# Output projection by one level of Strassen's scheme over pairs of token tiles, with more dense work left behind the attention

## The chip, the core and the metric

The kernel runs on one core of a Trainium2 chip. The metric is the time of one execution in microseconds on the device, lower is better. Before the change three runs took 998.38, 996.33 and 998.14 us, median 998.14. Engines are called as in the profile: PE (TensorE, matmuls), PEld (its weight loads), DVE (VectorE), ACT (ScalarE), POOL (GpSimd), and SP, whose queue issues nearly all DMAs.

## What is computed

Two independent halves over S = 2048 tokens and D = 576 features, written side by side to one output of 2048 x 1152, all in float32:

```python
# A: infini-attention, 32 heads of 18, four segments of 512 tokens
q, k, v = x @ wq, x @ wk, x @ wv
for s in range(4):                       # per segment and head
    p = softmax(qs @ ks.T * scale + mask)
    o_s = g * (phi(qs) @ M) / (phi(qs) @ z) + (1 - g) * (p @ vs)
    M, z = M + phi(ks).T @ vs, z + sum(phi(ks))
a = concat(o) @ wo                       # the output projection
# B: Fourier mixing by matrices
y = dft_seq_re @ (x @ dft_hid_re.T) - dft_seq_im @ (x @ dft_hid_im.T)
```

The mask lets a query see the keys at and before its own place.

## The kernel before

The order of all instructions on every engine is the order in which the program is written (manual_schedule). Two generators are woven into each other by hand: attention() yields a planned time for each slot of work (SLOTS), dense() yields a planned time for each few matmuls of half B, and the loop at the end of the kernel takes dense steps while the dense share of its total stays below the attention's share. total_a is the attention's planned time divided by 0.995, so that 0.5% of the dense plan is left when the attention has ended. later(n, fn) puts a call n ticks ahead; a tick passes at each attention slot, and "while due: tick()" empties the list.

Float32 products are made of three rounded ones: a value is split into hi (an ACT copy to fp32r) and lo (a subtraction raw - hi, on DVE or POOL), and hi x lo', hi x hi' and lo x hi' are summed in PSUM. Features come as four blocks of 128 and a tail of 64; the tail's hi and lo share one tile of 128 rows.

The stages in order: projections and memory (up to about 215 us), then attention woven with dense (to about 928 us), a rest of dense, then the output projection. For attention, each group of four heads is transposed by turn_out and written to the DRAM tile od, the last features of four groups by turn_tails to odt; both DMAs go through the SP queue. wo_load and wo_split bring in and split the weight wo in five row blocks during the last dense products (tt of 8 and more, ri = 1).

The output projection is a loop over 16 token tiles of 128 rows. o_load(t) brings tile t from od and odt with three DMAs, o_split(t) makes hi, lo and the tail, and for each half of the columns (288) a chain of 14 matmuls (4 blocks x 3, and 2 for the tail) runs into one PSUM bank, which ACT copies to SBUF (L1025); four DMAs store a tile. Tiles 0 and 1 are loaded inside attention(), at p == NP + 1; tile t + 2 is loaded when tile t is split. Its matmuls have line L84 in the profile (the helper chain), those of dense L583 and L628 to L634.

SBUF tiles come from pools with a number of buffers per tag. "wide" has 32 buffers (weights, and part of the dense intermediate), "ab" ten for the rest of it. sb2a holds the attention's tiles; open_output closes it and opens sb3 in its place.

Of the kernel before, what the change touches and what calls it, by code (L numbers as in the profile page):

```python
# [12 lines left out]
F32 = mybir.dt.float32  # L13
F32R = mybir.dt.float32r
# [3 lines left out]
OP = mybir.AluOpType  # L18
# [5 lines left out]
P = 128  # L24
# [16 lines left out]
def infini_attention_and_fnet(ctx: ExitStack, tc: tile.TileContext, xT, wqk, w8, wv, wo, beta, xtT, cT, hT, out):  # L41
# [13 lines left out]
    od = [dram.tile([4, 4 * P, P], F32, name=f"od{s}") for s in range(NSEG)]  # L55
    odt = [dram.tile([2 * P, P], F32, name=f"odt{s}") for s in range(NSEG)]

    def split(hi, lo, raw, lo_engine=None):
        act.activation(hi, raw, AF.Copy)
        (lo_engine or dve).tensor_tensor(lo, raw, hi.bitcast(F32), OP.subtract)  # L60
# [625 lines left out]
    O, O3, OT, WO, WORAW = {}, [], {}, [], []  # L686

    def o_load(t):  # L690
        if t >= NT:
            return
        s, a = divmod(t, 4)
        o = O3[0].tile([P, 5, P], F32, name="o", bufs=3) if O3 else sb.tile([P, 5, P], F32, name="raw", tag="raw", bufs=3)
        dma(o[:, :4], od[s][:, a * P:a * P + P].rearrange("c p x -> p c x"))
        for i in range(2):
            dma(o[64 * i:64 * i + 64, 4], odt[s][64 * a:64 * a + 64])
        O[t] = o

    def o_split(t):  # L700
        if t >= NT:
            return
        o_load(t + 2)
        o = O.pop(t)
        hi = O3[0].tile([P, 4, P], F32R, name="oth", bufs=2)
        lo = O3[0].tile([P, 4, P], F32R, name="otl", bufs=2)
        tl = O3[0].tile([P, P], F32R, name="ott", bufs=2)
        split(hi, lo, o[:, :4])
        act.activation(tl, o[:, 4], AF.Copy)
        dve.tensor_tensor(tl[64:], o[64:, 4], tl[64:].bitcast(F32), OP.subtract)  # L710
        OT[t] = hi, lo, tl

# [4 lines left out]

    def wo_split(k):
        if k == 0:
            WO.extend(weight(wide_tile(D)))  # L720
        split_wk(WO, k, WORAW.pop(0), 2)

    def open_output():
        p2a.close()
        O3.append(ctx.enter_context(tc.tile_pool(name="sb3", bufs=1, reuse_waits="tile")))

    p2a = ExitStack()
# [179 lines left out]
    def turn_tails(s, u):  # L907
        t = sa.tile([P, 4, 32], F32, name="oglt", bufs=1)
        dve.transpose(t, TAILS[-1])
        later(3, dma, odt[s].rearrange("(p u) x -> p u x", u=2)[:, u], t.rearrange("p q j -> p (q j)"))  # L910

# [9 lines left out]
    def attention():  # L921
        for p in range(NP + V_LAG):
# [90 lines left out]
    for t in range(NT):  # L1013
        o_split(t + 1)
        hi, lo, tl = OT.pop(t)
        y = O3[0].tile([P, D], F32, name="y3", bufs=2)
        for h in range(2):
            cs = slice(h * 288, h * 288 + 288)
            o = ps.tile([P, 288], F32, name="d", bufs=3)
            terms = []  # L1020
            wh, wl, wt1, wt2 = WO
            for k in range(4):
                terms += [(hi[:, k], wl[k][:, cs]), (hi[:, k], wh[k][:, cs]), (lo[:, k], wh[k][:, cs])]
            chain(o, terms + [(tl, wt1[:, cs]), (tl, wt2[:, cs])])
            act.activation(y[:, cs], o, AF.Copy)  # L1025
            if h or t == NT - 1:
                cs = cs if t == NT - 1 else slice(0, D)
                for q in range(4):
                    r = 512 * (t // 4) + P * q + 32 * (t % 4)
                    queue = nc.scalar if h and t == NT - 1 and q >= 2 else nc.sync  # L1030
                    queue.dma_start(out[r:r + 32, cs], y[32 * q:32 * q + 32, cs])

# [4 lines left out]
def _out_features():  # L1037


    f = np.arange(D).reshape(8, 72)  # L1040
    main = f[:, :64].reshape(4, 4, 32).transpose(0, 2, 1)
    return np.concatenate([main.ravel(), f[:, 64:].reshape(2, 32).T.ravel()])

# [29 lines left out]
```

## Time and profile before

| what | value |
|---|---|
| runs | 998.38, 996.33, 998.14 us, median 998.14 |
| profiled execution | span 996.2 us from first to last instruction; what lies outside the span isn't recorded |
| mean granted clock of PE | 0.999 |
| instructions | 25590 |
| DMA | 208.92 MB, mean 210 GB/s |

The page lists, for each engine, the time in which it was busy. A group row reads: line, engine, operation, output <- inputs, shapes, count | total busy us, mean ns of one | idle time just before, and what ended it. A window row gives the length of a stretch, then busy us (and instructions) of PE, PEld, DVE, ACT and POOL in it, the granted clock of PE, the share of DMA and GB/s. A timeline row is start, duration, engine, line, operation, output <- input. A matmul row's duration includes the pipeline behind it, so that the spacing of matmuls is read from how many end in a stretch. The "q" in SPq means the engine's queue, that is, issuing.

### The profile page before, as it was taken

The numbers are of one execution on the slowest core, as the hardware profiler recorded it, in microseconds if no ns is written. First come the engines' busy times: TensorE is split into PE (matmuls) and PEld (weight loads), VectorE is DVE, ScalarE is ACT, GpSimd is POOL, SyncE is SP. The second block draws the span as 40 slices with busy tenths as digits, with TensorE's granted clock in tenths as the row PEclk, the third lists the DMA queues.
The fourth block names the chain that finished last, engine by engine and source line by source line (L and its number), as shares of the span: only waits on it lengthen the run. The fifth ranks groups of instructions, "written<-read, shape, count | busy, mean of one in ns | idle before, by whom it ended". The sixth has DMA issues, their size and how long they took to land.

```text
span 996.2 us, 25590 instructions
## 1 busy us (share of the span) xinstructions
PE 986.1 (99%) x9294; PEld 924.1 (93%) x9294; DVE 753.5 (76%) x2052; ACT 712.0 (71%) x1680; POOL 636.3 (64%) x700
## 2 busy tenths in 40 slices
PE   9999999999999999999999999999999999999998
PEld 8989989899999999999999999999999999999998
DVE  6657667594678777888898888888889899998321
ACT  7757575653887877878788888877777787777243
POOL 2657676675767677666766777766766767667000
PEclk9999999999999999999999999999999999999999
DMA  7537456767588898899999988779999999989455
GB/s 252 187 117 257 172 180 242 234 232 228 150 174 217 215 251 222 207 237 215 245 238 238 222 214 199 178 200 226 230 216 229 238 235 242 240 191 200 128 148 142
DMA packets 305615, 208.92 MB, mean 210 GB/s; under 512 B 206289, under 2 KB 260433, under 8 KB 305489
## 3 DMA queue, kind: packets, MB, share of 16 engines
q1 hardware_dynamic: 305248, 207.15, 80.8%
q8 instruction: 73, 1.20, 0.5%
q14 instruction: 54, 0.43, 0.2%
q10 hardware_dynamic: 240, 0.14, 0.0%
HBM read 121.32 MB, written 57.93 MB: 180 GB/s over the span
## 4 chain that ended last, share of the span: by engine, by line
PE 84%; DVE 6%; ACT 5%; issue 2%; DMA 2%; POOL 1%; SPq 0%; POOLq 0%; DVEq 0%; ACTq 0%
PE d L583 38%; PE s L744 7%; PE d L84 6%; PE v L84 4%; PE pv L862 4%; PE qk L250 4%; PE d L628 3%; PE d L629 3%; PE d L630 3%; PE pv L863 2%; PE m L363 1%; PE t L818 1%; PE qk L84 1%; DVE r L276 1%; PE t L821 1%
## 5 line engine op out<-in xcount | busy, mean ns | idle before, releaser
L750 DVE CUSTOM_DVE_ANT_0 s<-s,causal 128x128 f32<-128x128 f32 (+3 forms) x512 | 248.1, 504 | 94.0 <-PE s L744 84.8
L456 POOL TENSOR_TENSOR clo<-craw,chi 128x512 fp32r<-128x512 f32 x158 | 217.1, 1374 | 94.4 <-ACT chi L451 66.4
L583 PE MATMUL d<-wide,chi 128*128 128x288 f32 x1408 | 261.7, 303 | 0.0
L583 PEld LDWEIGHTS d<-wide,chi 128*128 128x128 f32 x1408 | 210.7, 188 | 2.7 <-issue 1.1
L583 PE MATMUL d<-wide,clo 128*128 128x288 f32 x704 | 173.3, 313 | 0.0
L784 POOL TENSOR_TENSOR hl<-pf,hl 128x768 f16<-128x768 f32 x64 | 112.6, 1759 | 69.3 <-ACT hl L780 58.7
L830 ACT ACTIVATE phi<-t 128x384 f16<-128x384 f32 x128 | 61.8, 483 | 103.8 <-PE t L827 103.8
L744 PE MATMUL s<-ks,qs 108*128 108x128 bf16 (+3 forms) x512 | 132.8, 303 | 2.7 <-DVE negm L750 2.1
L773 ACT ACTIVATE pf<-s,nb 128x128 f32<-128x128 f32 (+3 forms) x256 | 128.3, 527 | 6.2
L583 PE MATMUL d<-ab,chi 128*128 128x288 f32 x640 | 123.3, 302 | 0.0
L845 DVE TENSOR_TENSOR plo<-pf,phi 128x384 f16<-128x384 f32 (+1 forms) x128 | 122.9, 960 | 0.0
L583 PEld LDWEIGHTS d<-wide,clo 128*128 128x128 f32 x704 | 117.8, 189 | 1.9 <-issue 0.5
L451 ACT ACTIVATE chi<-craw 128x512 fp32r<-128x512 f32 x160 | 100.2, 627 | 6.1 <-DMA craw<-xtT 3.3
L831 ACT ACTIVATE pf<-t 128x384 f32<-128x384 f32 (+1 forms) x192 | 99.5, 518 | 5.9 <-PE t L818 5.5
L583 PEld LDWEIGHTS d<-ab,chi 128*128 128x128 f32 x640 | 97.8, 189 | 0.5
L780 ACT ACTIVATE hl<-pf 128x768 f16<-128x768 f32 (+1 forms) x128 | 87.4, 729 | 2.0
L583 PE MATMUL d<-ab,clo 128*128 128x288 f32 x320 | 83.0, 308 | 0.0
L628 PE MATMUL d<-wide,chi 128*128 128x288 f32 x256 | 81.3, 318 | 0.0
L629 PE MATMUL d<-wide,chi 128*128 128x288 f32 x256 | 75.7, 296 | 0.0
L630 PE MATMUL d<-wide,clo 128*128 128x288 f32 x256 | 75.6, 295 | 0.0
L845 POOL TENSOR_TENSOR plo<-pf,phi 128x384 f16<-128x384 f32 x64 | 61.4, 959 | 13.8 <-ACT pf L831 13.3
L784 DVE TENSOR_TENSOR hl<-pf,hl 128x512 f16<-128x512 f32 x64 | 69.4, 1084 | 0.1
(214 smaller groups left out, 2500.1 us busy)
## 6 DMA issues: line engine op xcount, KB each, us to landing
craw<-cT SPq DMA_DIRECT2D x128, 256.0 KB
ks<-kd SPq DMA_DIRECT2D x32, 432.0 KB
qs<-qd SPq DMA_DIRECT2D x32, 432.0 KB
craw<-xtT SPq DMA_DIRECT2D x32, 320.0 KB
vd<-vs SPq DMA_DIRECT2D x16, 440.0 KB
vst<-vd SPq DMA_DIRECT2D x32, 220.0 KB
qd<-p SPq DMA_DIRECT2D x16, 384.0 KB
kd<-p SPq DMA_DIRECT2D x16, 384.0 KB
```

Of the source, the lines that this page charges most:

```text
L84: pe.matmul(o, a, b, start=n == 0, stop=n == len(terms) - 1)
L451: act.activation(hi, raw[:, :4], AF.Copy)
L456: engine.tensor_tensor(lo, raw[:, :4], hi.bitcast(F32), OP.subtract)
L583: pe.matmul(o[h], a, b[:, h * 288:h * 288 + 288], start=start, stop=stop)
L628: pe.matmul(o, xh[:, k], wl[k][:, cs], start=k == 0, stop=False)
L629: pe.matmul(o, xh[:, k], wh[k][:, cs], start=False, stop=False)
L630: pe.matmul(o, xl[:, k], wh[k][:, cs], start=False, stop=False)
L744: pe.matmul(o[:, c:c + w], q[:, i * P:w], k[:, :w], start=True, stop=True)
L750: dve.tensor_tensor_reduce(o[:, c:c + w], o[:, c:c + w], CAUSAL[0][:, L - w:], scale=scale, scalar=-LOWEST, op0=OP.add, op1=OP.min, accum_ ...
L773: act.activation(f[:, FIRST_COL[i]:FIRST_COL[i] + w], o[:, c:c + w], AF.Exp, bias=nb[:, i:i + 1], scale=-1.0)
L784: engine.tensor_tensor(hl[:, 1, a:b], f[:, a:b], hl[:, 0, a:b], OP.subtract)
L845: (pool if kind == 2 else dve).tensor_tensor(lo[:, a:b], f[:, a:b], hi[:, a:b], OP.subtract)
```

## The change

The projection takes token tiles n and n + 8 as one pair, and the two halves of the 576 input features (two blocks of 128 and 32 tail features each) and of the 576 output columns as the other two dimensions. It forms seven products (Strassen's scheme in Winograd's form) instead of eight:

P1 = A11 B11, P2 = A12 B21, P3 = S1 T1, P4 = S2 T2, P5 = S3 T3, P6 = S4 B22, P7 = A22 T4,

where S1 to S4 are sums and differences of blocks of the activations (rows n above, rows n + 8 below) and T1 to T4 of blocks of wo. Each product is a chain of seven matmuls of 288 columns: three for each of two feature blocks, and one for the tails, whose 96 rows hold hi, hi and lo against lo', hi' and hi'. Some products are added in PSUM on top of an earlier one after that has been read.

For this
- the host orders wo differently, in six blocks; wo_split makes B11, B21 and B22 from them;
- the tails of o are copied in DRAM from odt into a new tile ods, four times over, by one more DMA after each turn_tails;
- o_load moves from the attention to open_output and the projection, three DMAs a tile;
- late_weights loads wo again and forms T1 to T4 (LATE) in three rounds, and left(0) forms the activations' blocks of the first pair; both are issued between the steps of the dense rest;
- output_stage runs the seven products of pair n between those of its neighbours, and left(n + 1), for the next pair, is issued between them: on POOL three sums of 384 columns and three low parts of 64 rows, on DVE one difference of 384 columns and seven low parts of 256, on ACT seven copies of 256 and three for the tails; evacuations are two on ACT and five on DVE;
- 0.995 in total_a becomes 0.975.

```diff
-                if ri and 0 <= late < 5:
+                if ri and 0 <= late < 6:
                     wo_load(late)
-                if ri and 1 <= late < 6:
+                if ri and 1 <= late < 7:
                     wo_split(late - 1)
...
+    LATE = ["T2", "T1", "T3", "T4"]
...
+    def o_load(t):
+        s, a = divmod(t, 4)
+        o = O3[0].tile([P, 2, 3, P], F32, name="o", tag="o", bufs=5)
+        for k in range(2):
+            dma(o[:, k, :2], od[s][2 * k:2 * k + 2, a * P:a * P + P].rearrange("c p x -> p c x"))
+        dma(o[:, :, 2], ods[s][a].rearrange("u p x -> p u x"))
+        O[t] = o
+
+    def late_weights():
...
+        load(0)
+        yield
+        for c in range(3):
+            (b11, b12), (b21, b22) = ((r[:, :288], r[:, 288:]) for r in raws.pop(c))
+            t = O3[0].tile([P, 4, 288], F32, name="tt", tag="tmp", bufs=2)
+            pool.tensor_tensor(t[:, 1], b12, b11, OP.subtract)
+            dve.tensor_tensor(t[:, 2], b22, b12, OP.subtract)
+            yield
+            dve.tensor_tensor(t[:, 0], b22, t[:, 1], OP.subtract)
+            yield
+            pool.tensor_tensor(t[:, 3], b21, t[:, 0], OP.subtract)
+            if c < 2:
+                load(c + 1)
+            yield
+            hi = th[:, :, c] if c < 2 else ts
+            act.activation(hi, t, AF.Copy)
+            yield
+            if c < 2:
+                for i in (0, 2):
+                    dve.tensor_tensor(tl[:, i:i + 2, c], t[:, i:i + 2], th[:, i:i + 2, c].bitcast(F32), OP.subtract)
+                    yield
+            else:
+                dve.tensor_tensor(ts[:32], t[:32], ts[:32].bitcast(F32), OP.subtract)
+                yield
+
+    def left(n):
...
+        def main(name, raw):
+            m = new()
+            act.activation(m[:, :2], raw[:, :2], AF.Copy)
+            dve.tensor_tensor(m[:, 2:], raw[:, :2], m[:, :2].bitcast(F32), OP.subtract)
+            LEFT[n, name] = m
+
+        def stack(to, raw):
+            act.activation(to, raw, AF.Copy)
+            pool.tensor_tensor(to[64:], raw[64:], to[64:].bitcast(F32), OP.subtract)
...
+        pool.tensor_tensor(t[:, 0], two[:, 0], two[:, 1], OP.add)
+        main("A11", one[:, 0])
+        stack(sa_[:, :2], one[:, :, 2])
+        yield
+        pool.tensor_tensor(t[:, 1], t[:, 0], one[:, 0], OP.subtract)
+        main("S1", t[:, 0])
+        yield
+        dve.tensor_tensor(t[:, 2], one[:, 0], two[:, 0], OP.subtract)
+        main("S2", t[:, 1])
+        yield
+        pool.tensor_tensor(t[:, 3], one[:, 1], t[:, 1], OP.subtract)
+        main("S3", t[:, 2])
+        yield
+        stack(ss, t[:, :, 2])
+        main("A12", one[:, 1])
+        yield
+        main("A22", two[:, 1])
+        stack(sa_[:, 2], two[:, 1, 2])
+        yield
+        main("S4", t[:, 3])
+        yield
 
     def open_output():
         p2a.close()
         O3.append(ctx.enter_context(tc.tile_pool(name="sb3", bufs=1, reuse_waits="tile")))
+        for t in (0, 8):
+            o_load(t)
+
+    def strassen_product(o, n, x, w, first):
+        m, st = LEFT.pop((n, x)), LEFT.pop((n, x, "s"))
+        hi, lo, ws = WO[w]
+        terms = []
+        for c in range(2):
+            terms += [(m[:, c], lo[c]), (m[:, c], hi[c]), (m[:, 2 + c], hi[c])]
+        for i, (a, b) in enumerate(terms + [(st[:96], ws[:96])]):
+            pe.matmul(o, a, b, start=first and i == 0, stop=True, skip_group_check=True)
...
+        for n in range(8):
+            todo = [(first, n), (second, n), (sixth, n - 1), (third, n), (seventh, n - 1), (fourth, n), (fifth, n)]
+            if n == 7:
+                todo += [(sixth, n), (seventh, n)]
+            if n < 6:
+                o_load(n + 2)
+                o_load(n + 10)
+            prepare = left(n + 1) if n < 7 else iter(())
+            for fn, k in todo:
+                if k < 0:
+                    continue
+                piece = fn(k)
+                next(piece)
+                next(prepare, None)
+                next(piece, None)
...
-        later(3, dma, odt[s].rearrange("(p u) x -> p u x", u=2)[:, u], t.rearrange("p q j -> p (q j)"))
+        later(3, dma, odt[s][u], t.rearrange("p q j -> p (q j)"))
+        later(5, dma, ods[s][:, u].rearrange("b (r i) x -> b r (i x)", r=4),
+              odt[s][u].rearrange("(b r i) x -> b r (i x)", b=4, r=1).to_broadcast([4, 4, 32 * P]))
...
-            if p == NP + 1:
-                o_load(0)
-                o_load(1)
...
-    total_a = (NP + V_LAG) * sum(SLOTS) / 0.995
+    total_a = (NP + V_LAG) * sum(SLOTS) / 0.975
...
+    def before_output():
+        yield from left(0)
+        yield from late_weights()
+        o_load(1)
+        o_load(9)
+
+    ready = before_output()
     for t in d:
         tick()
-        td += t or 0.0
-        if 0 in O and td > total_d - 3000.0:
-            o_split(0)
+        next(ready, None)
     while due:
         tick()
...
+    for _ in ready:
+        pass
+    output_stage()
```

In output_stage, first(n) is P1, second is P4 (S2, T2), third P3, fourth P5, fifth P2, sixth P7, seventh P6; first and fifth are copied out by ACT, the others by DVE, and each pair's result goes out in eight DMAs.

More of the change, by code (lines that the diff above doesn't have):

```diff
@@ L55, in infini_attention_and_fnet @@
     od = [dram.tile([4, 4 * P, P], F32, name=f"od{s}") for s in range(NSEG)]
-    odt = [dram.tile([2 * P, P], F32, name=f"odt{s}") for s in range(NSEG)]
+    odt = [dram.tile([2, P, P], F32, name=f"odt{s}") for s in range(NSEG)]
+    ods = [dram.tile([4, 2, P, P], F32, name=f"ods{s}") for s in range(NSEG)]
     def split(hi, lo, raw, lo_engine=None):
@@ L679, in dense @@
                     h_split(1, late - 1)
-                if ri and 0 <= late < 5:
+                if ri and 0 <= late < 6:
                     wo_load(late)
-                if ri and 1 <= late < 6:
+                if ri and 1 <= late < 7:
                     wo_split(late - 1)
                 yield from sequence(ri, tt)
[L686 to L711, printed above, removed]
+    O, O3, LEFT, WORAW, Y3 = {}, [], {}, [], {}
+    WO = {}
+    LATE = ["T2", "T1", "T3", "T4"]
     def wo_load(k):
@@ new lines, in wo_split @@
+        a, b, stacks_ = WO["all"]
+        raw = WORAW.pop(0)
+        if not half:
+            raw = raw[:, :288]
+        if c < 2:
+            hi, lo = (b[0][c], b[1][c]) if half else (a[0][:, c], a[1][:, c])
+            act.activation(hi, raw, AF.Copy)
+            later(2, dve.tensor_tensor, lo, raw, hi.bitcast(F32), OP.subtract)
+        else:
+            st = stacks_[1] if half else stacks_[0][:, :288]
+            act.activation(st, raw, AF.Copy)
+            later(2, dve.tensor_tensor, st[:32], raw[:32], st[:32].bitcast(F32), OP.subtract)
@@ L1004, in infini_attention_and_fnet @@
     open_output()
+    def before_output():
[4 more added lines that the diff above has]
+    ready = before_output()
     for t in d:
         tick()
-        td += t or 0.0
-        if 0 in O and td > total_d - 3000.0:
-            o_split(0)
+        next(ready, None)
     while due:
         tick()
[L1013 to L1031, printed above, removed]
+    for _ in ready:
+        pass
+    output_stage()
 _INS = ("xT", "wqk", "w8", "wv", "wo", "beta", "xtT", "cT", "hT")
```

90 lines of the change are left out of this document (85 added, 5 removed).

## The prediction

> **What bounds the kernel now.** I read the busy times first, then the wait list of PE, then the same busy times by stretches of the span.
>
> ```profile
> PE 986.1 (99%) x9294; PEld 924.1 (93%) x9294; DVE 753.5 (76%) x2052; ACT 712.0 (71%) x1680; POOL 636.3 (64%) x700
> ```
>
> ```profile
> PE s L744 <- DVE negm L750: 2.1, 5, 0.8
> ```
>
> ```profile
> 800.00:900.00 100.00, 98.81 (x1066) 92.42 (x1064) 93.55 (x253) 77.31 (x178) 71.06 (x77) 1.00 0.91 219
> ...
> 920.00:940.00 20.00, 20.00 (x183) 19.86 (x183) 8.04 (x22) 4.34 (x11) 2.95 (x4) 1.00 0.44 119
> ...
> 980.00:990.00 10.00, 10.00 (x78) 10.00 (x77) 1.97 (x4) 3.80 (x10) 0.00 (x0) 1.00 0.59 155
> ```
>
> PE sets the time: its longest listed wait adds up to 2.1 us, so every matmul less is time less, as long as the others keep up. In a window row the columns are length, PE, PEld, DVE, ACT, POOL, clock. Late in the attention DVE is 94% busy; in the output projection DVE and ACT are 20% and 38% busy and POOL does nothing. The chain of waits then gives the two stretches that change:
>
> ```profile
> 928.01 4.33 PE d L583 x32
> 932.34 59.42 PE d L84 x448
> ```
>
> After the attention's last matmul 32 dense matmuls are left (4.33 us); then the projection's 448 take 59.42 us, so 0.1326 us each.
>
> **What it removes.** Eight pairs of tiles, seven products each, seven matmuls per product: 8 x 7 x 7 = 392 instead of 448, all 288 columns wide as before. 56 x 0.1326 = 7.4 us less. The projection's PE floor is 52.0 us, one product 0.93 us, one pair 6.5 us.
>
> **What it moves.** 0.995 becomes 0.975 in total_a, so 2% more of total_d (453.8 us by the code's own 120 ns and 95 ns) stays behind the attention: 9.1 us by that count, 76 matmuls of 120 ns, and 76 x 0.1326 = 10.0 us on the chip. From the attention's last matmul to the end of the dense products it is now 4.3 + 10.0 = 14.3 us. PE's work is only reordered, at no cost, while the attention can run the 10 us denser. DVE at 93.55 of 100 would go to about 95; I take 1 us of new waits (0 to 5, from the 1.2 us PE idles there now). The eight new transfers into ods each make SP wait for odt to land before the transposes and loads behind it can be issued; 8 x 1.8 us of queue. I price it at 0, since SP runs ahead of its consumers there; without that cover it is at most the 14 us. wo comes in six row blocks instead of five, three of them split over half their width: one load more, and no more work on ACT and DVE.
>
> **The first pair: what must happen in those 14.3 us.** Zero is the last attention matmul, at 927.83 here.
>
> ```profile
> 927.83 0.18 PE L863 MATMUL pv<-vst,ptt 128*128 128x37 bf16 x1
> ```
>
> ```profile
> 929.72 0.50 DVE L897 STREAM_TRANSPOSE ogt<-og 128x128 f32<-128x128 f32 x2
> 930.14 0.28 DVE L909 STREAM_TRANSPOSE oglt<-ogl 128x128 f32<-128x128 f32 x1
> ```
>
> ```profile
> 930.65 0.38 SPq L94 DMA_DIRECT2D odt<-oglt  x1
> 931.09 0.44 SPq L695 DMA_DIRECT2D o<-od  x1
> 931.58 1.15 SPq L697 DMA_DIRECT2D o<-odt  x2
> ...
> 971.38 0.38 SPq L695 DMA_DIRECT2D o<-od  x1
> 971.81 1.20 SPq L697 DMA_DIRECT2D o<-odt  x2
> 973.10 1.92 SPq L1031 DMA_DIRECT2D out<-y  x4
> ```
>
> ```profile
> 974.41 0.63 ACT L59 ACTIVATE oth<-o 128x512 fp32r<-128x512 f32 x1 [0.77 <-DMA o<-od]
> ```
>
> Before, tiles 0 and 1 were loaded during the attention. Now the first loads are written behind the attention's last transfers on the same SP queue: od, odt, and the new ods, which has to wait until odt has landed. A load lands 1.4 us after its issue ends (973.01 to 974.41, where ACT waited for it). So: odt issued by +3.2, landed +4.6, ods issued (0.4) +5.0, six issues for tiles 0 and 8 (two of 0.4 and one of 0.55 each, 2.7) +7.7, landed +9.1. Only then can POOL add the first two blocks. The durations:
>
> ```profile
> L653 DVE TENSOR_TENSOR y<-y,d 128x288 f32<-128x288 f32 x32 | 14.1, 445 | 2.2 <-PE d L583 2.2
> ...
> L60 DVE TENSOR_TENSOR otl<-o,oth 128x512 fp32r<-128x512 f32 x14 | 9.7, 692 | 38.6 <-ACT oth L59 38.6
> ...
> L710 DVE TENSOR_TENSOR ott<-o,ott 64x128 fp32r<-64x128 f32 x14 | 4.1, 289 | 1.2 <-ACT ott L709 0.8
> ```
>
> ```profile
> 917.51 1.29 POOL L456 TENSOR_TENSOR clo<-craw,chi 128x512 fp32r<-128x512 f32 x1
> ```
>
> ```profile
> L458 POOL TENSOR_TENSOR xtail<-craw,xtail 64x128 fp32r<-64x128 f32 x30 | 14.8, 492 | 2.4
> ```
>
> ```profile
> L780 ACT ACTIVATE hl<-pf 128x768 f16<-128x768 f32 x64 | 54.0, 844 | 2.0
> ...
> L1025 ACT ACTIVATE y<-d 128x288 f32<-128x288 f32 x32 | 12.8, 411 | 35.3 <-PE d L84 26.9 <-DMA out<-y 5.3 <-ACT ott L709 3.1
> ...
> L59 ACT ACTIVATE oth<-o 128x512 fp32r<-128x512 f32 x14 | 8.8, 628 | 3.2 <-DMA o<-od 3.2
> ```
>
> On straight lines through these, DVE takes 0.42, 0.46, 0.56, 0.76 and 1.36 us for 256, 288, 384, 576 and 1152 columns; POOL 0.49, 0.76, 0.82, 1.03, 1.29 for 128, 256, 288, 384, 512; ACT 0.41 for 256, 1.17 for 1152.
>
> - left(0) on POOL: three sums of 384 columns and stacks of 256, 512 and 128: 3 x 1.03 + 0.76 + 1.29 + 0.49 = 5.6. With 1.3 of waiting behind DVE (next part): +16.0.
> - late_weights, first block of rows: POOL 0.82, DVE 0.46, POOL 0.82: +18.1. The raw blocks are loaded by then.
> - The second block can't run beside the first, since the DVE queue holds its differences behind the first one's low parts: ACT 1.17, DVE 2 x 0.76, DVE 2 x 0.46, POOL 0.82 = 4.4: +22.5. The third likewise: +26.9. Then ACT 1.17 and DVE 1.36: +29.4.
>
> The product with S2 and T2 is second on PE, which reaches it at 14.3 + 0.93 = +15.2. It waits 14.2 us, and everything on PE is queued behind it. From both sides: all three blocks overlapped, POOL alone being the limit, is 9.1 + 5.6 + 6 x 0.82 + 2.5 = +22.1, a wait of 6.9; with no overlap at all of the three engines in left(0) (ACT and DVE add 4 us) about 18. I take 14.2, since each link is an in-order queue.
>
> **The other pairs: DVE and POOL exclude each other.**
>
> ```profile
> 810.79 1.65 POOL L784 TENSOR_TENSOR hl<-pf,hl 128x768 f16<-128x768 f32 x1 [0.19 <-ACT hl L780]
> 812.40 1.09 POOL L835 TENSOR_SCALAR_AFFINE_SELECT pf<-pf 128x512 f32<-128x512 f32 x1
> ```
>
> ```profile
> 811.00 1.99 DVE L845 TENSOR_TENSOR plo<-pf,phi 128x512 f16<-128x512 f32 x1
> ...
> 814.79 0.69 DVE L784 TENSOR_TENSOR hl<-pf,hl 128x512 f16<-128x512 f32 x1
> ```
>
> ```profile
> 907.33 0.63 POOL L835 TENSOR_SCALAR_AFFINE_SELECT pf<-pf 128x512 f32<-128x512 f32 x1
> ```
>
> A DVE difference of two SBUF tiles that takes 0.69 alone took 1.99 when it started under a POOL instruction: it ended 0.55 us after POOL did (812.44 to 812.99). The POOL instruction behind it took 1.09 instead of 0.63. They take turns, so their durations add up and don't overlap.
>
> One left(n) needs, of such work, DVE 7 x 0.42 + 0.56 = 3.5 and POOL 5.6: 9.1 us. Each hand-over gains 0.14 (0.55 against 0.69), at most 13 times, so 7.3 to 9.1; I take 8.4, nearer the upper end, because of the dependencies (sum, difference, copy, low part) between the three. The Trainium skill's page "SBUF — State Buffer", section "Who interferes with whom", speaks against the change more strictly: a VectorE instruction with two SBUF inputs and a GpSimd instruction that reads SBUF exclude each other, and the second is blocked until the first has wholly finished. By that no hand-over gains anything, 9.1 us per pair; the trace agrees on the exclusion and shows the 0.14 besides. PE needs 6.5 per pair. Alone, the engines would fit: POOL 5.6, DVE 3.5 + 5 x 0.45 = 5.75, ACT 5.0 (nine copies of at most 0.63 and two of 0.41). SP fits: six loads 2.7 and eight stores 3.8 make 6.5, all inside 8.4. left(1) starts when POOL has left the weights, at +26.9; left(7) ends at 26.9 + 7 x 8.4 = +85.7; the last pair has nine products, 8.4: +94.1. The stores behind the last product are as before.
>
> **The sum.** On the same zero the old projection would end at 14.3 + 59.4 = +73.7. Difference +20.4, in which the 7.4 us saved are contained. With 1 us for the denser attention and 1 for the clock:
>
> ```profile
> 994.00:995.00 1.00, 0.00 (x0) 0.00 (x0) 0.00 (x0) 0.00 (x0) 0.00 (x0) 0.92 0.19 55
> 995.00:996.20 1.20, 0.00 (x0) 0.00 (x0) 0.00 (x0) 0.00 (x0) 0.00 (x0) 0.50 0.00 0
> ```
>
> the clock falls to half about 3 us after the last matmul, so a 14 us wait loses it; the three products after it take up to 2.8 us longer, but PE is not the bound there; 0 to 2.8. The span would go from 996.2 to 1018.6. The page gives nothing outside the span; the runs lie 0.1 to 2.2 us above it, their median 1.9; 1018.6 + 1.9 = 1020.5, rounded to 1020.
>
> **Rivals.**
> - Preparation hidden (the other side). The loads aren't held behind odt: 2.7 of issue and 1.4 of landing make +4.1 instead of +9.1, and DVE and POOL run side by side, the three weight blocks too. Then T2 comes at 22.1 - 5 = +17.1, a wait of 1.9 against 7.4 saved: 998.1 - 5.5 = 992.6. It decides only if both hold; without the early loads the wait of 6.9 leaves 997.6, no change. For it: each engine alone is under 6.5 us per pair. Against it: the order on SP and the rows at 811.
> - Wait, but no exclusion: the output is bound by PE after +29.4. 998.1 + 14.2 - 7.4, with 1 for the attention: 1006. For it: hand-overs overlap; against it: 7.3 is still over 6.5.
> - Harder on both sides: 9.1 per pair (7 x 0.7 = 4.9 more) and 5 us instead of 1 lost in the denser attention, where DVE has 6% left: 1020 + 8.9 = 1029.
> - The clock doesn't come back. If the gaps of about 2 us in each pair keep it at 0.5, 55 products of 1.86 end at 29.4 + 102 = +132: 1057. Against it: in the rows above it held for 3 us of idleness. "TensorE: Matmul & The Clock Gate" of the Trainium skill, section "A second HAM failure mode: psum-queue depth-cycling", describes a kernel whose frequent short idles did cost it its clock; no run shown here has such gaps.
> - That it does less than it says: the count of 392 is in the loops, so only a wait can undo it.
>
> **How the numbers follow.** Forecast 0.59 (own range 1012, with 7.3 per pair, to 1026); no exclusion 0.16; harder 0.07; hidden 0.15 (0.12 faster, 0.03 no change); clock 0.03. 0.2%, or 2 us, is what these runs can tell from nothing. Faster 0.12, same 0.03, slower 0.85. The range takes in the forecast, the second and the third rival: 1003 to 1031.
>
> **What would show it.** 392 projection matmuls, still 0.13 us each where they are back to back. A PE wait of some 14 us before the second product, ended by DVE (ts), with the clock at 0.5 behind it. The first o load issued after ods. A period of about 8.4 us between first products, DVE differences of 256 columns at 0.42 free and over 0.8 under POOL. A period of 6.5 would prove the exclusion harmless; no long wait before T2 would prove the chain wrong, and both together the forecast.

## The result and the profile after

| | before | after |
|---|---|---|
| median of five runs beside each other | 998.05 us (996.33 to 998.38) | 1031.69 us (1029.87 to 1034.27) |
| ratio, 95% interval | | 1.0346 [1.0332, 1.036] |
| the profiled execution, its span | 996.2 us (span) | 1033.57 us, span 1031.9 |
| last attention matmul starts at | 927.83 us | 923.39 us |

The change makes the kernel 3.5% slower. The forecast was 1020.0, 22 us slower, with a range up to 1031; it came out 34 us slower, 0.7 us above the range. First the busy times of the page, then the list of PE's waits, both of the kernel after:

```profile
PE 990.2 (96%) x9238; PEld 922.6 (89%) x9238; DVE 804.4 (78%) x2135; ACT 721.4 (70%) x1715; POOL 689.1 (67%) x754
```

```profile
PE d L584 <- ACT chi L452: 13.0, 2, 10.6
PE t L824 <- DVE ts L763: 4.2, 1, 4.2
PE t L824 <- DVE u L859: 4.0, 6, 0.9
PE pv L1038 <- DVE plo L1020: 2.1, 1, 2.1
```

PE has 56 matmuls fewer (9294 to 9238) and yet more busy time, in part because some of them ran at half clock. DVE and POOL are 51 and 53 us busier. The list of waits, which had nothing above 2.1 us, now holds 13.0 us in the *dense* products (line 584), 4.2 us before the end of the projection's second product, and 4.0 us spread over the pairs.

The window rows answer to the 920 to 940 and 980 to 990 rows of before (columns: length, PE, PEld, DVE, ACT, POOL, clock):

```profile
930.00:940.00 10.00, 1.63 (x13) 1.40 (x11) 1.10 (x3) 1.25 (x3) 1.99 (x3) 0.78 0.62 193
940.00:950.00 10.00, 5.11 (x24) 4.53 (x24) 7.45 (x9) 4.68 (x10) 7.12 (x7) 0.71 0.35 94
950.00:960.00 10.00, 5.72 (x37) 5.03 (x37) 5.78 (x9) 2.60 (x5) 5.94 (x6) 0.97 0.25 73
960.00:970.00 10.00, 8.54 (x46) 8.19 (x47) 9.01 (x15) 5.04 (x16) 6.77 (x7) 0.69 0.59 174
...
980.00:990.00 10.00, 9.23 (x67) 8.75 (x67) 9.41 (x18) 5.62 (x17) 6.75 (x8) 1.00 0.57 155
```

From 930 to 960 PE executes 74 matmuls, which back to back would take 10 us; DVE and POOL are both near idle for the first 10 us of it and are busy for 5.8 to 7.5 us of each 10 afterwards. Where the pairs run (980 to 990), DVE is busy 9.41 of 10 us, POOL 6.75, and the clock is full.

PE's timeline shows what it waited in. These are the rows of the start-up:

```profile
942.21 1.33 PE L584 MATMUL d<-wide,chi 128*128 128x288 f32 x4 [10.57 <-ACT chi L452]
943.84 0.85 PE L584 MATMUL d<-wide,clo 128*128 128x288 f32 x2 [0.31 <-POOL clo L457]
...
950.07 0.79 PE L584 MATMUL d<-ab,chi 128*128 128x288 f32 x4 [2.45 <-ACT chi L452]
...
961.18 0.61 PE L824 MATMUL t<-ts,x 96*128 96x288 f32 x1 [4.19 <-DVE ts L763]
```

The 14.3 us of dense matmuls that were to cover the preparation stood still themselves. Their last two operands are still to be cut when the attention ends (high part on ACT, line 452, low part on POOL, line 457), and the loop that issues the dense steps advances left(0) and late_weights by one piece per step, so these cuts stand in the ACT and POOL queues *behind* preparation pieces that wait for the o loads. The same on POOL and on ACT:

```profile
937.85 0.99 POOL L789 TENSOR_TENSOR ss<-o 128x384 f32<-128x384 f32 x1 [10.96 <-DMA o<-ods]
...
942.23 1.56 POOL L457 TENSOR_TENSOR clo<-craw,chi 128x512 fp32r<-128x512 f32 x1 [0.20 <-ACT chi L452]
...
950.10 1.33 POOL L457 TENSOR_TENSOR clo<-craw,chi 128x512 fp32r<-128x512 f32 x1 [1.79 <-ACT chi L452]
```

```profile
935.63 0.42 ACT L774 ACTIVATE x<-o 128x256 fp32r<-128x256 f32 x1 [13.73 <-DMA o<-od]
...
941.54 0.61 ACT L452 ACTIVATE chi<-craw 128x512 fp32r<-128x512 f32 x1
...
949.41 0.61 ACT L452 ACTIVATE chi<-craw 128x512 fp32r<-128x512 f32 x1
```

SP's queue shows why the loads were late:

```profile
927.92 0.41 SPq L95 DMA_DIRECT2D odt<-oglt  x1
929.74 0.68 SPq L95 DMA_DIRECT2D ods<-odt  x1
930.47 0.94 SPq L725 DMA_DIRECT2D o<-od  x2
...
933.07 0.47 SPq L726 DMA_DIRECT2D o<-ods  x1
```

SP waited for odt to land, as forecast, issued ods at 929.74 and then the loads of tiles 0 and 8; the last issue ended at 933.54. But POOL began only at 937.85, so this load took 4.3 us to land, not the 1.4 us of the row that the forecast used.

The queue was late before that too. The issue of odt ended 4.9 us after the start of the last attention matmul (928.33 after 923.39), where the forecast had 3.2, as in the kernel before. DVE shows why:

```profile
924.50 0.45 DVE L654 TENSOR_TENSOR y<-y,d 128x288 f32<-128x288 f32 x1 [6.19 <-PE d L584]
924.87 0.21 DVE L1050 RECIPROCAL pv<-pv 128x8 f32<-128x8 f32 x1
```

With the denser weaving a subtraction of the dense product, which waits for PE, stands in DVE's queue ahead of the attention's last normalisation (line 1050). That starts 1.48 us after the last attention matmul; in the kernel before it was 0.22 (928.05 after 927.83). A second such subtraction (line 654, at 926.54) comes ahead of the transposes. Experiment 11, where only the weaving is denser, has the same two; experiment 1, with the old weaving, has odt's issue end at +3.2.

**Where the 35.7 us of span went.** Each line is measured minus forecast, from the rows here and in the prediction:

| stretch | forecast | measured | difference |
|---|---|---|---|
| last attention matmul, due at 927.83 − 10.0 = 917.83 | +1 | 923.39: +5.6 | +4.6 |
| from there to T2 complete (the ts matmul at 961.18) | 29.4 | 37.8 | +8.4 |
| from there to the last matmul's end (1023.25) | 64.7 | 62.1 | −2.6 |
| from there to the end of the span | 4.5, as before | 8.65 | +4.2 |
| clock, counted apart | 1 | within the others | −1 |

The sum is 13.6 us, against 1031.9 − 1018.6 = 13.3. The two rows of the last stretch, the end of PE's work before (991.74 of 996.2) and after:

```profile
991.32 0.42 PE L84 MATMUL d<-wide,ott 128*128 128x288 f32 x2
```

```profile
1022.15 1.10 PE L824 MATMUL d<-wide 128*128 128x288 f32 x7
...
1020.91 8.94 SPq L831 DMA_DIRECT2D out<-yo  x12
```

The SP row merges 12 stores and hides a wait among them. SP's own list of waits (total, times, longest; from 1012 us on) has it, and SP's and ACT's timelines behind it show the stores that were left:

```profile
SPq L831 <- DMA out<-yo: 3.5, 1, 3.5
```

```profile
1025.35 4.51 SPq L831 DMA_DIRECT2D out<-yo  x10
```

```profile
1023.77 0.82 ACTq L831 DMA_DIRECT2D out<-yo  x2
```

SP stood for 3.5 us until another store had landed, and then issued ten stores at 0.45 us each. By the trace's semaphores the store it waited for is one of the last two, which ACT's queue issued at 1023.77. Eight of SP's ten had their data by 1022.81.

### The profile page after: what moved, and what is told of

It reads as the page before. It is cut to its first block, busy times and chain, and to the rows that moved or that the text cites. A ratio compares the mean times of both kernels' runs of the same rounds, so it can differ in the third digit from the quotient of the medians.

```text
span 1031.9 us, 25691 instructions
## 1 busy us (share of the span) xinstructions
PE 990.2 (96%) x9238; PEld 922.6 (89%) x9238; DVE 804.4 (78%) x2135; ACT 721.4 (70%) x1715; POOL 689.1 (67%) x754
## 4 chain that ended last, share of the span: by engine, by line
PE 74%; DVE 8%; ACT 6%; issue 4%; DMA 3%; POOL 3%; SPq 1%; POOLq 0%; DVEq 0%; ACTq 0%
PE d L584 34%; PE s L919 7%; PE v L85 4%; PE pv L1037 4%; PE qk L251 4%; PE d L629 3%; PE d L630 3%; PE d L631 3%; PE pv L1038 2%; PE m L364 1%; PE t L993 1%; PE qk L85 1%; DVE r L277 1%; ACT qe L220 1%; DMA craw<-xtT 1%
## 5 line engine op out<-in xcount | busy, mean ns | idle before, releaser
L584 PEld LDWEIGHTS d<-wide,chi 128*128 128x128 f32 x1408 | 212.6, 190 | 13.6 <-ACT chi L452 10.8
L1020 POOL TENSOR_TENSOR plo<-pf,phi 128x384 f16<-128x384 f32 x64 | 60.9, 951 | 16.4 <-ACT pf L1006 13.6
L959 DVE TENSOR_TENSOR hl<-pf,hl 128x512 f16<-128x512 f32 x64 | 64.3, 1005 | 0.0
```

Of the source, the lines that this page charges most:

```text
L584: pe.matmul(o[h], a, b[:, h * 288:h * 288 + 288], start=start, stop=stop)
L959: engine.tensor_tensor(hl[:, 1, a:b], f[:, a:b], hl[:, 0, a:b], OP.subtract)
L1020: (pool if kind == 2 else dve).tensor_tensor(lo[:, a:b], f[:, a:b], hi[:, a:b], OP.subtract)
```

## The experiments

Theory: the excess over the old time is four things. A: the attention loses about 5 us by being denser. B: a chain of preparation holds up PE at the start, about 38 us from the last attention matmul to T2. C: DVE and POOL exclude each other, which makes a pair 7.8 us instead of 6.5. D: the store queue adds 4 us at the end, in which that wait of SP is 3.5. The main rival to B: the rest of dense work held back in front of the chain is what costs, and clear issue order would hide the preparation. "T2 complete" below is the start of the matmul that reads ts, counted from the last attention matmul of the same profile, unless it says otherwise. The kernel before ran beside each, at medians between 997.5 and 998.4. In the profiles of kernels with the same denser attention its last matmul fell anywhere from 919.96 to 926.87 us, so a difference of 2 us between two of these kernels says nothing unless the trace has its place.

**1. No denser attention** (after, with the old factor):

```diff
-    total_a = (NP + V_LAG) * sum(SLOTS) / 0.975
+    total_a = (NP + V_LAG) * sum(SLOTS) / 0.995
```

> Only total_a goes back from 0.975 to 0.995. Chain theory (everything behind the attention's last matmul hangs on one chain of loads, left(0) and late_weights that starts there, so that the last attention matmul sets the end and not the amount of dense rest): the last attention matmul comes near 927.5 instead of 923.4, 4 us later; the two cuts of craw for the dense rest, which stood in the middle of the chain, fall away and give 3 to 4 back; 1031 to 1035 us. Density theory (the denser attention itself loses the time): 5 to 6 us less, 1026. Cover theory (the rest hides the preparation): 10 us more, 1042.

1035.36 us, ratio 1.0367 [1.0352, 1.0383], 0.4 us above what the chain theory expected. The attention ends at 928.15, as before within 0.3 us, and T2 comes at 963.43 (+35.3). PE's waits in this kernel:

```profile
PE t L824 <- DVE tl L760: 14.7, 2, 11.5
PE s L824 <- ACT x L774: 6.1, 1, 6.1
```

The wait is longer and lies in the projection itself. So the 10 us of dense work moved behind the attention are worth 3.7 us by the medians, 2.1 by the ratios, whose intervals just overlap: the chain B is there with or without it.

**2. The dense rest first** (no piece of the preparation until all dense steps are issued):

```diff
     for t in d:
         tick()
-        next(ready, None)
```

> The whole dense rest is issued ahead of left(0) and late_weights, nothing else is changed. Chain theory: PE no longer waits for the craw copies (13 us in the profile), the rest ends near 938, but the product with T2 still waits for the chain, which gets shorter by the two POOL subtractions of craw and the wait for their ACT copies only: 3 to 5 us less, 1027 to 1029. Rival (the 13 us in which PE stood in the dense rest are themselves the loss): 1018 to 1020.

1028.14 us, 1.029 [1.0273, 1.0307], as expected. The rest runs without a gap and its last matmul starts 14.3 us after the last attention matmul (935.83 after 921.53), but PE then stands in the second product:

```profile
947.41 0.61 PE L824 MATMUL t<-tl,x 128*128 128x288 f32 x1 [9.41 <-DVE tl L760]
...
951.67 0.61 PE L824 MATMUL t<-tl,x 128*128 128x288 f32 x1 [3.18 <-DVE tl L760]
...
956.52 0.61 PE L824 MATMUL t<-ts,x 96*128 96x288 f32 x1 [3.76 <-DVE ts L763]
```

T2 complete at +35.0 instead of +37.8. The rest standing still was a symptom: with the rest ahead, the same wait stands behind it, one for each row block of T2. It is this picture that the prediction had drawn, with 16.4 us of waits in place of 14.2.

**3. No late weights** (the four T's replaced by blocks of wo that exist, so the sums of weights aren't made):

```diff
-        yield from late_weights()
+        for n, b in zip(LATE, ("B11", "B21", "B22", "B11")):
+            WO[n] = WO[b]
+        yield
```

> late_weights is left out; T1 to T4 are taken to be blocks of wo that are there already, so the products are those of other matrices. Chain theory: no wait for T; the pairs start when the dense rest and left(0) are done, near 949 to 951 instead of 961, and take their 62 us as before: 1020 to 1022. If the exclusion of DVE and POOL alone set the time, so that left(1) to left(7) would be late anyway: over 1028.

1022.55 us, 1.0237 [1.0222, 1.0252]: 9 us off the kernel after, just over what was expected. PE still stands 10.3 us in the dense rest (`ACT chi`), which is the loads' part of B; the weights' part is the 9 us.

**4. POOL without reads** (in left(1) to left(7) each POOL sum and low part is replaced by two memsets of the same output, so these operands are constants):

```diff
+        def sums(to, a, b, op):
+            if n == 0:
+                pool.tensor_tensor(to, a, b, op)
+            else:
+                for _ in range(2):
+                    pool.memset(to.bitcast(F32), 0.25)
...
-        pool.tensor_tensor(t[:, 0], two[:, 0], two[:, 1], OP.add)
+        sums(t[:, 0], two[:, 0], two[:, 1], OP.add)
```

> In left(1) to left(7) every POOL sum and low part is replaced by two memsets of the same tile, which write and don't read, and keep POOL about as busy; the values are then constants. Exclusion theory: DVE's 256-column subtractions take 0.42 throughout instead of up to 1.4, a pair takes 6.5 to 6.8 us instead of 7.8, the whole 7 to 9 us less: 1023 to 1025. Rival (the pace comes from the dependencies among the three engines, or from SP): a pair stays over 7.5 us and the time within 2 us of 1031.7.

1026.4 us, 1.0274 [1.0255, 1.0292]. The DVE groups by line from the first pair on, first of the kernel after, then of this one (count, busy time, mean ns):

```profile
L775 DVE TENSOR_TENSOR wide<-ss,wide 128x256 fp32r<-128x256 f32 x28 | 18.2, 651 | 0.6 <-ACT wide L774 0.2
L775 DVE TENSOR_TENSOR wide<-o,wide 128x256 fp32r<-128x256 f32 x21 | 17.9, 853 | 1.8 <-ACT wide L774 1.8
L796 DVE TENSOR_TENSOR ss<-o 128x384 f32<-128x384 f32 x7 | 7.0, 1005 | 0.0
```

```profile
L782 DVE TENSOR_TENSOR wide<-ss,wide 128x256 fp32r<-128x256 f32 x28 | 11.8, 420 | 8.0 <-ACT wide L781 7.7
L782 DVE TENSOR_TENSOR wide<-o,wide 128x256 fp32r<-128x256 f32 x21 | 8.8, 420 | 3.4 <-ACT wide L781 3.4
L803 DVE TENSOR_TENSOR ss<-o 128x384 f32<-128x384 f32 x7 | 3.9, 550 | 0.3 <-issue 0.3
```

With POOL no longer reading, every one of the 49 differences takes 0.42 us; beside a reading POOL they took 0.65 and 0.85 on average. The period between pairs (from one third product, P3, to the next) fell from 7.8 to between 6.5 and 6.6 for five intervals, PE's own 6.5, and was 7.8 again in the last. The memsets also wait for no input, so part of the shorter period can come from a shorter chain of dependencies; the shorter DVE durations can't. So DVE is slowed by the exclusion, and the engines have time enough.

What then set the last interval is SP's queue. It issued each pair's six loads and eight stores without a pause, and took 6.9 to 7.0 us for them (loads begin at 984.07, 991.11 and 997.97), more than PE's 6.5, until a load came late and held up ACT. By these rows a pair without the exclusion would settle near 7 us, an estimate:

```profile
1002.49 0.42 ACT L786 ACTIVATE wide<-o 128x256 fp32r<-128x256 f32 x1 [1.75 <-DMA o<-ods]
```

From T2 to the last matmul's end it is 54.1 us instead of 62.1, but SP's wait among the last stores grew from 3.5 to 4.9 us, about as much as the 1.4 us above the upper expectation.

**5. Loads ahead of ods** (experiment 2, and the last ods transfer held back until the preparation is issued):

```diff
-        later(5, dma, ods[s][:, u].rearrange("b (r i) x -> b r (i x)", r=4),
-              odt[s][u].rearrange("(b r i) x -> b r (i x)", b=4, r=1).to_broadcast([4, 4, 32 * P]))
+        copy = (dma, ods[s][:, u].rearrange("b (r i) x -> b r (i x)", r=4),
+                odt[s][u].rearrange("(b r i) x -> b r (i x)", b=4, r=1).to_broadcast([4, 4, 32 * P]))
+        if s == 3 and u == 1:
+            HELD.append(copy)
+        else:
+            later(5, *copy)
...
+        for fn, *a in HELD:
+            fn(*a)
```

> On top of e2 (dense rest first, 1028.1): the last transfer into ods is held back until left(0) and late_weights have been issued, so that the first o loads no longer stand behind it. Chain theory: 1.4 us of waiting for odt, 0.7 of issue and up to 3 of slow landing beside its 16 KB packets fall away, POOL's first sum starts about 9 us after the last attention matmul instead of 14.5, and all that hangs on it comes 4 to 5 us sooner: 1023 to 1024.5. If the loads land late whatever stands ahead of them: within 1.5 us of 1028.

1029.21 us, 1.0312 [1.0281, 1.0343]: no gain, where 4 us or more were expected. One half held: POOL's first sum began 10.3 us after the last attention matmul (926.87) instead of 14.1 in experiment 2. The other half is in DVE's timeline:

```profile
940.70 0.45 DVE L654 TENSOR_TENSOR y<-y,d 128x288 f32<-128x288 f32 x1 [9.64 <-PE d L584]
...
941.88 0.42 DVE L775 TENSOR_TENSOR x<-o,x 128x256 fp32r<-128x256 f32 x1
```

With the whole rest issued first, its subtraction from PSUM (line 654) stands in DVE's queue ahead of left(0), and it waits for PE to finish the rest. DVE idled 9.64 us, for the last 3.5 of them with all blocks landed. The attention also ended late in this profile, 5 us after that of experiment 2.

**6. Four last stores on ACT's queue** (experiment 2, first half of the last tile):

```diff
-            queue = nc.scalar if last and q >= 2 else nc.sync
+            queue = nc.scalar if first or last and q >= 2 else nc.sync
...
-                store(n, Y3[n][0], C)
+                store(n, Y3[n][0], C, first=True)
```

> On top of e2: four of the last pair's twelve stores (those of the fifth product) are issued by ACT's queue instead of SP's. Theory of the tail (between the last matmul and the end lie 8.6 us instead of 4.4, because SP issues one store in about half a microsecond and has some ten of them behind the last products): 2 us less, 1026. Rival (the stores are late by their data): no change.

1026.0 us, 1.0279 [1.0258, 1.0301], 2.1 us under experiment 2, as expected, though the two intervals overlap. From the end of PE's work to the end of the span it is 7.3 us instead of 8.6 (1023.2 − 1015.9 against 1026.4 − 1017.8), so 1.3 us of D were SP's queue of these four stores; its wait stays, at 3.7 us. In this profile the attention ended 1.6 us earlier besides.

**7. Two more POOL operations on DVE** (experiment 2; in left(n), n ≥ 1, the first sum and the low part of the stacked S tails):

```diff
-        pool.tensor_tensor(t[:, 0], two[:, 0], two[:, 1], OP.add)
+        (dve if n else pool).tensor_tensor(t[:, 0], two[:, 0], two[:, 1], OP.add)
...
-        stack(ss, t[:, :, 2])
+        stack(ss, t[:, :, 2], dve if n else pool)
```

> On top of e2: in left(1) to left(7) one of POOL's three sums and its 512-column low part go to DVE, which does both in less time (0.56 + 0.69 against 1.03 + 1.29). Exclusion theory: the time in which the two need the shared path falls from 9.1 to 8.0 us per pair, DVE's own work rises from 5.75 to 7.0; a pair takes about 7.2 instead of 7.83, 3 to 5 us less: 1023 to 1025. Rival (DVE is simply the busier engine and sets the pace): more work on DVE makes a pair longer, over 8.5, 1033 or more.

1027.78 us, 1.0287 [1.0257, 1.0318]. The period is 7.35 instead of 7.82, close to the 7.2 expected: work is shorter on DVE, and a POOL operation that is gone excludes nothing. The time as a whole missed: in the profile the attention ended at 923.89, 2.4 us after that of experiment 2, and hid most of the gain, which was 2.2 us from T2 to the last matmul's end (59.1 instead of 61.3).

**8. Weights ahead of left(0)** (experiment 5; half of the reload of wo goes out during the last dense product but one, late_weights runs first):

```diff
+                if ri and late == 6:
+                    for i in range(3):
+                        later(4 + i, early_load, i)
...
-        yield from left(0)
-        yield from late_weights()
+        yield from late_weights()
+        yield from left(0)
```

> On top of e5: half of the second load of wo goes out some 10 us sooner, during the last dense product but one, and late_weights is issued ahead of left(0), into the time in which the engines waited for the o loads. Chain theory: late_weights starts about 3 us after the last attention matmul and is done 13 to 14 us later, left(0) overlaps its end; the second product comes near 942 instead of 956.5, and the whole takes 1013 to 1017. If the preparation weren't one serial chain from the loads on: no less than e5, 1023.

1029.66 us, 1.0313 [1.0289, 1.0337]: no gain, where 1013 to 1017 was expected. It is experiment 5's fault again, and now it holds up the weights: DVE waited 9.64 us for the same subtraction, and PE waited 12.2 us for left(0) (`ACT x L772`).

**9. The cuts first, then the preparation** (experiment 5, with the preparation issued right behind the rest's last cut, so ahead of its subtractions):

```diff
-    for t in d:
+    for i, t in enumerate(d):
         tick()
+        if i == 17:
+            for _ in ready:
+                pass
```

> As e5, but the preparation isn't behind the whole dense rest: it is issued once the rest's last cut of craw has been issued, so that DVE's preparation stands ahead of the two last subtractions of the dense product, which wait for PE. In e5 DVE stood 9.6 us in front of those. Chain theory: POOL's first sum about 10 us after the last attention matmul, T2 ready 20 to 21 us later, at +31 instead of +35 in e2: 4 us less than e2, 1023 to 1025. If the first loads don't carry the chain: 1027 or more.

1024.79 us, 1.0275 [1.0261, 1.0289], as expected. T2 complete at +31.0 (953.09 after 922.14), the expected place:

```profile
943.98 0.61 PE L824 MATMUL t<-tl,x 128*128 128x288 f32 x1 [6.32 <-DVE tl L760]
...
948.24 0.61 PE L824 MATMUL t<-tl,x 128*128 128x288 f32 x1 [3.17 <-DVE tl L760]
...
953.09 0.61 PE L824 MATMUL t<-ts,x 96*128 96x288 f32 x1 [3.76 <-DVE ts L763]
```

So both parts of experiment 5's reading hold: the loads' 4 us are there once no queue has something late in front of the chain. The prediction had +29.4, but with 1.8 us for ods in front of the loads, which this kernel doesn't have there: like for like it is +31.0 against +27.6. Of these 3.4 us, 2.8 lie ahead of POOL's first sum (+10.1 against +7.3) and 0.6 in the preparation itself (20.9 against 20.3).

**10. Cuts first, weights ahead of left(0)** (experiments 8 and 9 together):

> As e8 (late_weights ahead of left(0), its first loads sooner), with the order of e9, so that DVE is free for it. Chain theory: the weights start on POOL about 7 us after the last attention matmul, behind the last cuts, are done near +20, and left(0) makes S2 and its tail by +24 to +26; the second product ends near 947 instead of 956.9 in e2: 1017 to 1020. If it stays over 1025, the start isn't one chain that can be begun sooner.

1022.57 us, 1.0256 [1.0242, 1.027], 2.6 us above what was expected. The weights start at +6.8 and are ready about 20 us after the last attention matmul; left(0) is now last, and PE waits for it:

```profile
943.46 0.85 PE L828 MATMUL s<-wide,x 128*128 128x288 f32 x2 [4.54 <-ACT x L772]
```

Its 14th product matmul is at +25.6 (949.89 after 924.33), where +24 to +26 was expected; what was missed is that the attention ended 2.2 us later in this profile than in experiment 9's, and that the second product's evacuation then waits longer (`DVE u L853`, 3.0 us).

**11. The kernel before, denser attention alone**:

```diff
-    total_a = (NP + V_LAG) * sum(SLOTS) / 0.995
+    total_a = (NP + V_LAG) * sum(SLOTS) / 0.975
```

> The kernel before with 0.975 in total_a and nothing else of the change: the attention woven denser, 10 us more of dense work behind it, projection as it was. Density theory (the attention, run denser, meets waits of DVE and POOL on each other and loses 3 to 5 us of PE's time and clock): 1000 to 1003. Rival (order costs nothing, what was lost there in the changed kernel comes from the new transfers): 997.5 to 999.

1002.76 us, 1.0055 [1.0042, 1.0067], as expected: denser weaving costs about 5.5 us by itself (0.0055 of 997.5), with nothing of Strassen in it. Its chain of waits shows the dense rest, 108 matmuls instead of 32, run through without a gap, so that nothing is lost behind the attention:

```profile
922.77 14.42 PE d L583 x108
937.19 59.43 PE d L84 x448
```

The loss lies in the attention. One piece of it has a place, the same in the kernel after, whose DVE and POOL rows near 532 us are:

```profile
530.32 1.86 DVE L127 TENSOR_TENSOR wide<-raw,wide 64x576 fp32r<-64x576 f32 x1
532.21 2.11 DVE L128 TENSOR_TENSOR wide<-raw,wide 64x576 fp32r<-64x576 f32 x1
...
534.35 1.01 DVE L1020 TENSOR_TENSOR plo<-pf,phi 128x512 f16<-128x512 f32 x1
```

```profile
530.30 1.27 POOL L457 TENSOR_TENSOR clo<-craw,chi 128x512 fp32r<-128x512 f32 x1 [2.38 <-ACT nb L945]
531.77 1.93 POOL L959 TENSOR_TENSOR hl<-pf,hl 128x768 f16<-128x768 f32 x1 [0.20 <-ACT hl L955]
533.66 1.16 POOL L1010 TENSOR_SCALAR_AFFINE_SELECT pf<-pf 128x512 f32<-128x512 f32 x1
```

Two low parts of a weight load, 576 columns each (0.76 us by the prediction's line), took 1.86 and 2.11 us between POOL's reads; the low part of the attention behind them came late, and PE idled 2.1 us at 533.3, the `plo` wait of the list. In the kernel after and in this one the clock was at 0.5 for 3.4 us afterwards. That is up to 2.1 + 1.7 = 3.8 us of the 5; the rest has no single place.

**12. All that helped** (experiments 10, 7 and 6 together):

> All parts together: e10, with one sum and one low part moved to DVE (e7) and the last pair's first stores on ACT's queue (e6). If the parts add: 1018.5 less 3.3 (seven periods of 7.35 instead of 7.83) less 2: 1011 to 1015, still over the 998 of before, since a pair takes 7.35 us here against 7.43 by the plain scheme and the start-up wait is not gone.

1017.55 us, 1.0204 [1.0189, 1.022], 2.5 us above what was expected, but 5.0 us under experiment 10 (5.3 expected), so the miss is experiment 10's. It is 14 us better than the change as made, and 20 us slower than the kernel before. None of the kernels tried beats the kernel before. Of experiment 12's 19.7 us of span (1015.9 against 996.2), the dense products end 4.4 us later than before (936.7 against 932.3) and the stretch behind them is 15.3 us longer (79.2 against 63.9), though its eight pairs at 7.35 us take no longer (58.8) than the 448 plain matmuls (59.4). What remains is the start-up and the stores.

## Why the prediction came out as it did

*The direction held, and the mechanism in its outline.* 392 projection matmuls at 0.13 us back to back; a first pair that waits for T2, though 13.0 us of PE's wait lay in the dense rest and only 4.8 before the second product; pairs set by DVE and POOL; a clock that falls to 0.5 and comes back. The rivals "preparation hidden" and "no exclusion" are out: experiments 2 and 9 have the wait, experiment 4 the exclusion. "The clock doesn't come back" is out: it was at 0.5 from 935.5 to 945.7 and from 959.4 to 966.2, and full from there to the end of PE's work.

*"Harder on both sides" came nearest in time (1029), but half by the wrong price.* Its 5 us for the denser attention were right; its 9.1 us per pair weren't.

1. **The denser attention, forecast 1 us: about 5.** The term failed in size. It was read from DVE's mean share (93.55 of 100, to 95 at most), and a mean says nothing of a place where two DVE operations and POOL's reads meet. Experiment 11 measures it alone. The transfers into ods, priced at nothing within the attention, cost nothing there that shows (experiment 1 has them and ends the attention as before).
2. **The first pair's chain, forecast +29.4: +37.8.** 5.4 of the 8.4 us lie ahead of POOL's first sum (+14.5 against +9.1), and the first failed steps are there. "odt issued by +3.2": it was +4.9, because of the dense subtractions ahead of it on DVE. "A load lands 1.4 us after its issue ends": the loads behind ods took 4.3 us, and 2.1 to 2.3 without ods (experiments 5 and 9). The row that the 1.4 was read from names the load from od, whose issue had ended at 971.76, so it can as well be read as 2.65 us. Issuing ods and the loads took 0.7 us more than allowed. The other 3.0 us lie between POOL's first sum and T2 (23.3 us against 20.3), and the step that failed there is "from the attention's last matmul to the end of the dense products it is now 14.3 us", as if this rest were only PE's: two of its operands were still to be cut on ACT and POOL, in the queues of the preparation. With the cuts out of its way the same stretch takes 20.9 us (experiments 2 and 9), so they cost 2.4, and the cover stood still for 13 us. The sum of the preparation's own durations was right within 0.6 us.
3. **The pairs, forecast 8.4: 7.8, and 8.0 on the average of the seven intervals.** Right mechanism, size off by 0.4 to 0.6. The term was 9.1 of work that excludes itself, less hand-overs; the value was taken too near the upper end of 7.3 to 9.1. Why a pair comes out below it isn't measured. One interval of 8.6 has a late load in it (POOL waited 1.1 us for it at 992.48). "SP fits", 6.5 us of issues per pair, holds beside 7.8, but the 6.5 is 6.9 to 7.0 where SP runs without a pause (experiment 4).
4. **The stores, forecast "as before": +4.2 us.** Failed by being priced at nothing. SP stood 3.5 us in a wait for another store, with ten stores still behind it; every kernel here with the new projection has this wait (3.5 us, 3.7 in experiments 6 and 12, 4.9 in experiment 4). No experiment takes the wait out, so its worth is argued from the trace; experiment 6 takes 1.3 us back by moving four of the stores.
5. **The clock, 1 us:** not separable; 17 us at half speed fell mostly in waits.

Terms 1, 2 and 4 erred in the same direction, together 17 us, term 3 gave 2.6 back. The range's upper end had taken in the harder pairs and the denser attention, but no chain longer than +29.4 and nothing for the stores.

## What to carry to other kernels

Before work is called cover for a preparation, list what that work still needs from *every* engine and where those instructions stand in each in-order queue; one instruction with a late operand in front of the chain, in either direction, undoes the plan (experiments 2, 5 and 9 differ in nothing but order). A row that merges many issues can hide a wait among them: the last 12 stores looked like 0.75 us each and were 0.45 us each and one wait. Scheme by scheme, a saving in matmuls has to be set against the elementwise work that it costs: here 56 matmuls (7.4 us) against eight DVE and six POOL operations per pair on operands that exclude each other, so that a pair took 7.8 us where two plain tiles took 7.4. A density near 94% of an engine that isn't the bound is not room of 6% for PE's neighbours; try the weaving alone before its gain is counted.

## What the runs showed of the hardware that wasn't expected

- The clock was at 0.5 for 3.4 us after only 2.1 us without a matmul (the kernel after at 536.2, and experiments 3, 4, 5, 7 and 9 to 12, with the same idle); in experiments 2, 6 and 8, with the same wait of 2.1 us, it stayed at 1. The forecast held it to be safe for 3 us. The Trainium skill's page "TensorE: Matmul & The Clock Gate", section "HAM oscillation — how this bites in real kernels", names idle gaps of more than about 3.4 us as what to avoid; here half clock followed a gap of 2.1 us in nine profiles of twelve. The kernel before and experiment 1, which have no such gap there, kept the full clock; why three profiles with the gap kept it too isn't known.
- A transfer from DRAM to DRAM in front of loads delays them long after its issue: with ods ahead, POOL's first sum started 4.0 to 4.3 us after the last load's issue (the kernel after, experiments 1, 2, 6 and 7), without it 2.1 to 2.3 us (930.15 to 932.24 in experiment 9, 934.87 to 937.21 in experiment 5).
